# Pooling sums of q, k and v: one tensor_reduce each on VectorE in place of two additions each on GpSimd, in an attention and feed-forward kernel

## The chip, the cores and the metric

The kernel runs on one core of one Trainium2 chip. The metric is the device time of one execution in microseconds (us), lower is better. Times come from unprofiled runs, in rounds in which the kernels that are compared follow one another on the same chip; a profiled execution gives the trace from which all durations below are read. The core has a matrix engine (TensorE, PE in the rows; PEld is its weight load), VectorE (DVE), ScalarE (ACT), GpSimd (POOL), and SyncE (SP), whose queue here issues nearly all DMA transfers. Each engine works through its own queue in order and waits on semaphores for the others.

## The reference

The program is an attention followed by a token mix and a feed-forward layer, in fp32, for 8 batches, 8 heads, 576 positions and a head width of 64:

```python
# attention; factor = 4, Sd = 144
q_d = q.reshape(B, H, Sd, factor, D).mean(axis=3)      # the same for k_d and v_d
out_d = sm_attn(q_d, k_d, v_d)                         # softmax attention of the 144 pooled positions
out_up = np.repeat(out_d, factor, axis=2)
mask = np.abs(pos[:, None] - pos[None, :]) < factor    # local attention: 7 neighbours
out_local = softmax(where(mask, scale * q @ k.T, -1e9)) @ v
x = (out_up + out_local).transpose(0, 2, 1, 3).reshape(B, S, H * D)     # 8 x 576 x 512
# token mix of rank 32, then the feed-forward layer, 512 -> 2048 -> 512
u = x + (x.transpose(0, 2, 1) @ U @ V).transpose(0, 2, 1)
return u + np.maximum(u @ w_ch1, 0.0) @ w_ch2
```

The pooled means of q, k and v are where the change is: sums of four neighbouring positions (the factor 1/4 is folded in later).

## The kernel before, in words

**Products.** Every large product is done with operands split in a high and a low part (names ending in H and L), three matmuls for one: H by H, L by H, H by L. W1 and W2 are split on the chip: 32 chunks of 128x512 come in raw, and `convert` makes the two parts with seven instructions each (L341 and L351 on ACT, L342, L344, L347 and L349 on DVE, L354 on POOL); U goes the same way after the last chunk of W2.

**Work items.** A "pair" is two heads of one batch; there are 32, four for each batch. The first five ("early") use TensorE for most of their pooled and local attention, in buffers that later hold W2. The other 27 ("late") go through `late_global`: it loads q and k with the head width on the partitions (`gq`, `gT`, 128 x 576) and v in a grouped form (`vr`, 72 partitions x 2 x 4 x 64, one load for each head), sums fours into `smq`, `smk` (128x144) and `vs` (72x128), makes scores, softmax and the upsampled output, while `local_attn` does the seven-neighbour part on POOL (the product `Pt`, L799) and DVE (its sum over neighbours, L804). `mix_part` takes the output of a pair through U (`ps_hu`, L848) and V (`ps_u`, L863) into u, whose parts `uH` (ACT) and `uL` (POOL, L871) the feed-forward layer reads. Of the late pairs, pairs 5, 6 and 7 belong to batch 1, whose first pair is pair 4, an early one.

**Feed-forward.** For each batch, two tiles of 288 positions and 16 chunks of the hidden width: 12 matmuls into `ps_h` (L888), ACT makes `hH` (L895), DVE makes `hL` (L896), and three steps later 12 matmuls add into four accumulators (`acc`, L911). 256 such steps in all.

**What sets the order.** All instructions are first given to a planner, a list scheduler with a cost for each instruction, a priority for each (ten times the pair's number, with offsets) and the number of buffers of each tile. It fixes the order on every engine; the engines then run these fixed queues, and only semaphores decide when something starts. So a change of one instruction's engine or cost moves others on all engines. `hL` has the first place on DVE among what is ready. `gq`, `gT`, `vr` have one buffer each, `vs` two; so the load for a later pair waits until the sums of the pair before have read the buffer (and, for `gq` and `gT`, until its scores have).

**What the change touches.** For a late pair, `pool_halves` (L412 to L418) adds pairs of q, then pairs of these sums, in two POOL additions through a buffer `gh`; it does the same for k. For v, L510 adds in place (72x256), L512 adds the rest (72x128). That is eight POOL additions a pair:

Of the kernel before, what the change touches and what calls it, by code (L numbers as in the profile page):

```python
# [16 lines left out]
ALU = mybir.AluOpType  # L17
AX = mybir.AxisListType
# [35 lines left out]
class Plan:  # L54
# [6 lines left out]
    def buf(self, pool, shape, dt, name, tag=None, bufs=1):  # L61
        return Buf(self, pool, shape, dt, name, tag or name, bufs)

    def op(self, eng, dur, fn, r=(), w=(), prio=0.0, after=(), lat=None, move=0.0, at=0.0):
        o = Op()
        o.eng, o.dur, o.fn, o.prio, o.succ, o.ndep, o.ready = eng, dur, fn, prio, [], 0, at
        o.lat, o.move = LATENCY[eng] + SLACK * (SLACK_FROM <= prio < 1000) if lat is None else lat, move
        deps = set(after)
        bufs = []
        for k in r:  # L70
            b = k[0] if isinstance(k, tuple) else k
            bufs.append(b)
# [129 lines left out]
def attn_mix_ffn_kernel(ctx: ExitStack, tc, q, kp, vp, qT, kT, v, U, Ub, V, w1, w2, mask, band, eye, pat, pool, vw, vn, ident, outT):  # L202
    nc = tc.nc
    B, H, S, D = q.shape
    HP = H // 2
    NPOS = 9
    SPAD = kp.shape[2]
# [29 lines left out]
    op, buf = plan.op, plan.buf  # L237
# [30 lines left out]
    def pool_tt(n, fn, r, w, prio, ns=2.11, after=()):  # L268
        return op(POOL, 0.147 + n * ns / 1000.0, fn, r, w, prio, after)
# [29 lines left out]
    def ring(shape, name, n=2):  # L299
        if name not in kept:  # L300
            tiles = [early_pool.tile([128, *shape], F32, name=f"{name}{i}") for i in range(n)]
            for t in tiles:
                nc.vector.memset(t[:], 0.0)
            kept[name] = [0, [Kept(t) for t in tiles]]
        r = kept[name]
        r[0] += 1
        return r[1][(r[0] - 1) % n]
# [12 lines left out]
    for _ in range(2):  # L320
        m = kept_tile([NS, 2, KW], "ms_b")
        op(POOL, 0.4, lambda m=m: nc.gpsimd.tensor_copy(
            out=m()[:, :, :, KL:KW].rearrange("p r h k -> p (r h) k"),
            in_=pat_sb.unsqueeze(1).broadcast_to([128, 2 * NS, KW - KL])), ["pat"], [(m, "pat")], 0.1)
# [78 lines left out]
    def work(is_early, pool, shape, dt, name, tag=None, bufs=1):  # L403
        if is_early:
            return buf(early_pool, shape, dt, name, tag, 2)
        return buf(pool, shape, dt, name, tag, bufs)
# [5 lines left out]
    def pool_halves(raw, lo, out, e, prio):  # L412
        gh = work(e, glo, [128, SD, 2], F32, "gh")
        x4 = lambda: raw()[:, lo:lo + S].rearrange("p (j r) -> p j r", r=4)
        pool_tt(2 * SD, lambda: nc.gpsimd.tensor_tensor(
            out=gh(), in0=x4()[..., 0:2], in1=x4()[..., 2:4], op=ALU.add), [raw], [gh], prio, 1.65)
        pool_tt(SD, lambda: nc.gpsimd.tensor_tensor(
            out=out(), in0=gh()[..., 0], in1=gh()[..., 1], op=ALU.add), [gh], [out], prio, 1.75)  # L418

    def early_global(b, hp, up_s, prio, qt, kt, vn):  # L420
        sq = work(True, glo, [128, SD], F32, "smq")
        sk = work(True, glo, [128, SD], F32, "smk")
# [11 lines left out]
        vs = ring([4 * D], "vs_e")  # L434
# [13 lines left out]
        for hh in range(2):  # L448
            p = ps[hh]
            mx = work(True, glo, [QH, 2], F32, "mx")  # L450
            dve(288, lambda p=p, mx=mx: nc.vector.tensor_reduce(
                out=mx(), in_=view(p, SD), axis=AX.X, op=ALU.max), [p], [mx], prio)
# [14 lines left out]
        for hh in range(2):  # L467
# [13 lines left out]
            def a_mm(ET=ET, pa=pa, v=vsx[hh]):  # L481
# [6 lines left out]
                out=od()[:QH, 2 * hh:2 * hh + 2, :], in0=view(pa, D),  # L488
                in1=ri()[:, hh, :].unsqueeze(2).broadcast_to([QH, 2, D]), op=ALU.mult), [pa, ri], [(od, hh)], prio)
        for hh in range(2):  # L490
            dma(lambda hh=hh: nc.sync.dma_start(
                out=up_s()[hh].rearrange("(a p) d -> p a d", a=2), in_=od()[:, 2 * hh:2 * hh + 2, :]),
                [(od, hh)], [(up_s, hh)], prio, 40)

    def late_global(b, hp, up_s, prio):
        h0 = 2 * hp
        g = lambda shape, name, bufs=1: buf(glo, shape, F32, name, None, bufs)
        sq, sk = g([128, SD], "smq"), g([128, SD], "smk")
        qr, kr = g([128, S], "gq"), g([128, SPAD], "gT")
        load_t(qr, qT, b, h0, prio)  # L500
        load_t(kr, kT, b, h0, prio)
        pool_halves(qr, 0, sq, False, prio)
        pool_halves(kr, (SPAD - S) // 2, sk, False, prio)
        vss = []
        for hh in range(2):
            x, vs = g([QH, 2, 4, D], "vr"), g([QH, 2, D], "vs", 2)
            vss.append(vs)
            dma(lambda hh=hh, x=x: nc.sync.dma_start(
                out=x(), in_=v[b, h0 + hh].rearrange("(a p r) d -> p a r d", a=2, r=4)), [], [x], prio, 150)
            pool_tt(256, lambda x=x: nc.gpsimd.tensor_tensor(  # L510
                out=x()[:, :, 0:2, :], in0=x()[:, :, 0:2, :], in1=x()[:, :, 2:4, :], op=ALU.add), [x], [x], prio)
            pool_tt(128, lambda x=x, vs=vs: nc.gpsimd.tensor_tensor(  # L512
                out=vs(), in0=x()[:, :, 0, :], in1=x()[:, :, 1, :], op=ALU.add), [x], [vs], prio)
        s_s = buf(dram, [2, S, KL + 1], F32, "s_s", bufs=4)
        ps = late_scores(qr, kr, sq, sk, s_s, prio - 0.4)
        rs, rr, ri = (g([QH, 4], n) for n in ("rs", "rr", "ri"))
# [1 line left out]
        for hh in range(2):  # L518
            mx, nb = g([QH, 2], "mx", 2), g([QH, 2], "nb", 2)
            dve(288, lambda hh=hh, mx=mx: nc.vector.tensor_reduce(  # L520
                out=mx(), in_=pooled_view(ps[hh]), axis=AX.X, op=ALU.max), [ps[hh]], [mx], prio)
# [24 lines left out]
        out = lambda: pa()[:QH, :4 * D].rearrange("p (a d) -> p a d", a=4)  # L546

        def a_mm():
# [8 lines left out]
            out=od(), in0=out(), in1=ri().unsqueeze(2).broadcast_to([QH, 4, D]), op=ALU.mult), [pa, ri], [od], prio)  # L557
# [10 lines left out]
    def load_t(t, src, b, h0, prio):  # L568
        dma(lambda: nc.sync.dma_start(out=t(), in_=src[b, h0:h0 + 2].rearrange("h d s -> (h d) s")),
            [], [t], prio)  # L570
# [480 lines left out]
```

## Time and profile before

| | |
|---|---|
| median of the runs before | 1037.44 us (1034.21 to 1039.74, 3 runs) |
| profiled execution, its own time | 1038.36 us |
| its span | 1036.6 us |
| TensorE busy | 996.9 us (96%), mean granted clock 0.981 |
| VectorE busy | 529.8 us (51%), 1054 instructions |
| GpSimd busy | 557.2 us (54%), 567 instructions |
| ScalarE busy | 388.0 us (37%) |

How to read rows: a row of a group gives line, engine, operation, output<-input, shapes, count, then busy microseconds and the mean nanoseconds of one, then the idle time ahead of them and what ended it. A row of the windows view gives a stretch of the span, its length, then for each engine the busy microseconds (with the number of instructions), the granted TensorE clock (1.00 is full speed), the busy share of the DMA engines and GB/s. A row of a timeline gives start, duration, engine, line, operation, and in brackets the idle time before it with what it waited for. A row of the waits gives who waits, for what, total microseconds, how often, and the longest.

The span has three stages: the first 83 us (weights W1, the early pairs), the stretch from 83 to 168 us (W2 and U are loaded and converted, the feed-forward layer of batch 0 begins), and the long rest, in which the remaining batches follow one another.

### The profile page before, as it was taken

How to read it: one execution, taken by the hardware profiler on the slowest of the kernel's cores; microseconds unless marked ns; L12 is line 12 of the kernel's file. 1: busy time of each engine (PE TensorE's matmuls, PEld its weight loads, DVE VectorE, ACT ScalarE, POOL GpSimd, SP SyncE). 2: the span in 40 equal slices, each digit the busy share in tenths (PEclk: the TensorE clock that was granted, in tenths of full speed). 3: DMA queues.
4: the chain of work that ended last, by engine and by line, in shares of the span. 5: the costliest groups of instructions: out<-in, count | busy, mean ns of one | idle time of the engine just before them, and what ended most of it. 6: DMA issues, size and time to landing. Idle time of an engine off the chain costs nothing.

```text
span 1036.6 us, 26946 instructions
## 1 busy us (share of the span) xinstructions
PE 996.9 (96%) x10831; PEld 975.3 (94%) x10831; DVE 529.8 (51%) x1054; ACT 388.0 (37%) x1234; POOL 557.2 (54%) x567
## 2 busy tenths in 40 slices
PE   6778898999999999999999999999999999999998
PEld 5667888999999999999999999999999999999998
DVE  5997898655554545444475344534652544211111
ACT  3676554442443434443344244423443232111110
POOL 4854568788575656565585638762765625211010
PEclk9896999999999999999999999999999999999999
DMA  8866764753555545545555355624644242000000
GB/s 279 226 172 179 199 186 116 149 138 104 135 137 115 141 113 132 128 86 146 120 137 125 87 132 133 143 75 101 151 116 117 64 113 50 24 1 24 1 24 23
DMA packets 222612, 120.30 MB, mean 116 GB/s; under 512 B 175492, under 2 KB 198456, under 8 KB 222488
## 3 DMA queue, kind: packets, MB, share of 16 engines
q1 hardware_dynamic: 222488, 118.58, 45.5%
q8 instruction: 85, 1.39, 0.6%
q14 instruction: 39, 0.32, 0.1%
HBM read 87.78 MB, written 30.75 MB: 114 GB/s over the span
## 4 chain that ended last, share of the span: by engine, by line
PE 84%; DVE 7%; POOL 3%; issue 2%; DMA 2%; ACT 2%; SPq 0%; DVEq 0%; POOLq 0%; ACTq 0%
PE acc L911 36%; PE ps_h L888 35%; PE ps_a L552 2%; PE ps_b L719 2%; DVE c L347 2%; PE ps_hu L848 1%; DVE c L349 1%; PE ps_t L539 1%; DMA w2r<-in_W 1%; PE ps_b L726 1%; POOL Pt L799 1%; DVE c L342 1%; DVE c L344 1%; PE ps_a L484 1%; PE ps_v L431 1%
## 5 line engine op out<-in xcount | busy, mean ns | idle before, releaser
L911 PE MATMUL acc<-hH,W2H 128*128 128x288 f32 x1024 | 310.5, 303 | 0.0
L896 DVE SCALAR_TENSOR_TENSOR hL<-ps_h,hH 128x288 fp32r<-128x288 f32 x256 | 116.6, 455 | 378.6 <-ACT hH L895 378.0
L888 PE MATMUL ps_h<-uH,W1H 128*128 128x288 f32 x1024 | 304.3, 297 | 4.1 <-DVE hL L896 3.1
L911 PE MATMUL acc<-hH,W2L 128*128 128x288 f32 x1024 | 303.1, 296 | 2.6 <-POOL W2L L354 2.6
L888 PE MATMUL ps_h<-uL,W1H 128*128 128x288 f32 x1024 | 303.4, 296 | 1.2 <-POOL uL L871 1.2
L911 PE MATMUL acc<-hL,W2H 128*128 128x288 f32 x1024 | 302.6, 296 | 0.0
L888 PE MATMUL ps_h<-uH,W1L 128*128 128x288 f32 x1024 | 302.0, 295 | 0.0
L799 POOL TENSOR_TENSOR Pt<-vl,at 128x896 f32<-128x896 f32 (+1 forms) x135 | 233.4, 1809 | 115.1 <-DVE acc L804 61.1
L895 ACT ACTIVATE hH<-ps_h 128x288 fp32r<-128x288 f32 x256 | 105.1, 410 | 433.6 <-PE ps_h L888 433.5
L888 PEld LDWEIGHTS ps_h<-uH,W1H 128*128 128x128 f32 x1024 | 193.5, 189 | 5.4 <-DVE hL L896 3.8
L911 PEld LDWEIGHTS acc<-hH,W2L 128*128 128x128 f32 x1024 | 193.2, 189 | 3.5 <-POOL W2L L354 3.5
L888 PEld LDWEIGHTS ps_h<-uL,W1H 128*128 128x128 f32 x1024 | 193.4, 189 | 1.5 <-POOL uL L871 1.5
L911 PEld LDWEIGHTS acc<-hH,W2H 128*128 128x128 f32 x1024 | 193.3, 189 | 1.1
L888 PEld LDWEIGHTS ps_h<-uH,W1L 128*128 128x128 f32 x1024 | 193.7, 189 | 0.0
L911 PEld LDWEIGHTS acc<-hL,W2H 128*128 128x128 f32 x1024 | 193.7, 189 | 0.0
L804 DVE TENSOR_REDUCE acc<-Pt 128x128 f32<-128x1024 f32 (+1 forms) x135 | 144.7, 1103 | 4.7 <-POOL Pt L799 2.3
L871 POOL TENSOR_TENSOR uL<-xT,uH 128x288 fp32r<-128x288 f32 x56 | 44.1, 811 | 71.3 <-ACT uH L869 71.2
L921 POOL TENSOR_TENSOR o<-uH,uL 128x288 f32<-128x288 f32 x64 | 49.8, 816 | 54.2 <-DMA out_t<-o 54.2
L840 POOL TENSOR_TENSOR xL<-xL,xH 116x640 fp32r<-116x640 f32 x28 | 44.0, 1572 | 64.2 <-ACT xH L839 49.3
L510 POOL TENSOR_TENSOR vr<-vr 72x256 f32<-72x256 f32 x54 | 42.4, 785 | 46.9 <-DMA vr<-in_v 46.8
L793 ACT ACTIVATE Pt<-ul 128x128 f32<-128x128 f32 (+1 forms) x135 | 48.4, 441 | 21.3 <-DVE acc L804 20.0
L744 ACT ACTIVATE se<-ps_b 96x114 f32<-96x114 f32 x108 | 38.5, 357 | 47.1 <-PE ps_b L719 34.1
(129 smaller groups left out, 1106.9 us busy)
## 6 DMA issues: line engine op xcount, KB each, us to landing
vl<-in_vp SPq DMA_DIRECT2D x54, 240.0 KB
out_t<-o SPq DMA_DIRECT2D x64, 144.0 KB
w1r<-in_W SPq DMA_DIRECT2D x16, 512.0 KB
w2r<-in_W SPq DMA_DIRECT2D x16, 512.0 KB
Y<-x_s SPq DMA_DIRECT2D x112, 72.0 KB
gT<-in_kT SPq DMA_DIRECT2D x27, 291.0 KB
xL<-x_s SPq DMA_DIRECT2D x28, 280.0 KB
gq<-in_qT SPq DMA_DIRECT2D x27, 288.0 KB
```

The source lines that it names most:

```text
L510: pool_tt(256, lambda x=x: nc.gpsimd.tensor_tensor(out=x()[:, :, 0:2, :], in0=x()[:, :, 0:2, :], in1=x()[:, :, 2:4, :], op=ALU.add), [x], ...
L744: act(n * KL, lambda p=ps[hh], se=se, n=n, rows=rows: nc.scalar.activation(se()[rows, 0:n].rearrange("p r k -> p (r k)"), p()[rows, 0:n * ...
L793: act(n * D, lambda n=n, ps=ps, Pt=Pt: nc.scalar.activation(Pt()[:, :n, :, 7], ul()[:, ps, :], AF.Copy), [ul], [(Pt, 1)], prio, 0.16)
L799: nc.gpsimd.tensor_tensor(out=Pt()[:, :n, :, 0:7].rearrange("p s d o -> p o s d"), in0=win, in1=at()[:, ps, :].rearrange("p s o -> p o s") ...
L804: dve(8.5 * n * D, lambda n=n, ps=ps, Pt=Pt: nc.vector.tensor_reduce(out=acc()[:, ps, :], in_=Pt()[:, :n], axis=AX.X, op=ALU.add), [(Pt, 0 ...
L840: pool_tt(640, lambda: nc.gpsimd.tensor_tensor(out=xL(), in0=xL().bitcast(F32), in1=xH().bitcast(F32), op=ALU.subtract), [xL, xH], [xL], prio)
L871: pool_tt(TN, lambda uH=uH, uL=uL, uf=uf: nc.gpsimd.tensor_tensor(out=uL()[:, hp, :], in0=uf(), in1=uH()[:, hp, :].bitcast(F32), op=ALU.su ...
L888: nc.tensor.matmul(ps()[:, :TN], w[:, dc, fs], u()[:, dc, :], start=(n == 0), stop=(n == 3 * NDC - 1))
L895: last_h[i] = act(TN, lambda: nc.scalar.activation(hH(), ps()[:, :TN], AF.Relu), [ps], [hH], FIRST, 0.05)
L896: dve(TN, lambda: nc.vector.scalar_tensor_tensor(hL(), ps()[:, :TN], 0.0, hH().bitcast(F32), op0=ALU.max, op1=ALU.subtract), [ps, hH], [hL ...
L911: nc.tensor.matmul(ac[e]()[:, :TN], W2[w][:, fc, es], hx(), start=(fc == 0 and n == 0), stop=(fc == NFC - 1 and n == 2))
L921: pool_tt(TN, lambda e=e, o1=o1: nc.gpsimd.tensor_tensor(out=o1()[:, :TN], in0=uH()[:, e, :].bitcast(F32), in1=uL()[:, e, :].bitcast(F32), ...
```

## The change

For late pairs the two additions of q, of k and of each head's v become one VectorE instruction, a `tensor_reduce` that sums the innermost four elements: 128x144 from 128x576 for q and for k, 72x128 from 72x512 for each v (its view is permuted so that the four summed are innermost, 64 elements apart in the buffer). Early pairs keep `pool_halves`. The planner is told 576 and 512 elements as their cost on DVE.

```diff
+    def sum_fours(raw, lo, out, prio):
+        dve(S, lambda: nc.vector.tensor_reduce(
+            out=out(), in_=raw()[:, lo:lo + S].rearrange("p (j r) -> p j r", r=4), axis=AX.X, op=ALU.add),
+            [raw], [out], prio)
...
-        pool_halves(qr, 0, sq, False, prio)
-        pool_halves(kr, (SPAD - S) // 2, sk, False, prio)
+        sum_fours(qr, 0, sq, prio)
+        sum_fours(kr, (SPAD - S) // 2, sk, prio)
...
-            pool_tt(256, lambda x=x: nc.gpsimd.tensor_tensor(
-                out=x()[:, :, 0:2, :], in0=x()[:, :, 0:2, :], in1=x()[:, :, 2:4, :], op=ALU.add), [x], [x], prio)
-            pool_tt(128, lambda x=x, vs=vs: nc.gpsimd.tensor_tensor(
-                out=vs(), in0=x()[:, :, 0, :], in1=x()[:, :, 1, :], op=ALU.add), [x], [vs], prio)
+            dve(512, lambda x=x, vs=vs: nc.vector.tensor_reduce(
+                out=vs(), in_=x().rearrange("p a r d -> p a d r"), axis=AX.X, op=ALU.add), [x], [vs], prio)
```

Lines behind the new function are numbered five higher in the changed kernel, and three higher from the end of the v sums on: L804 becomes L807, L848 L851, L863 L866, L888 L891, L896 L899, L911 L914; the new reduces are L421 (q and k) and L515 (v).

Since the planner orders everything anew, the queues differ in more than the replaced rows. Three places follow.

VectorE, while W2 is converted (`c_...` is a chunk's working copy), the conversion of one chunk. Before:

```order
L342 TENSOR_SCALAR c_1867<-c_1867 128x512
L344 TENSOR_SCALAR c_1867<-c_1867 128x512
L347 SCALAR_TENSOR_TENSOR c_1867<-w2r,c_1867 128x512
L896 SCALAR_TENSOR_TENSOR hL<-ps_h,hH 128x288
L349 SCALAR_TENSOR_TENSOR c_1867<-w2r,c_1867 128x512
L342 TENSOR_SCALAR c_1942<-c_1942 128x512
```

Now:

```order
L342 TENSOR_SCALAR c_1869<-c_1869 128x512
L344 TENSOR_SCALAR c_1869<-c_1869 128x512
L515 TENSOR_REDUCE vs<-vr 72x128
L899 SCALAR_TENSOR_TENSOR hL<-ps_h,hH 128x288
L347 SCALAR_TENSOR_TENSOR c_1869<-w2r,c_1869 128x512
L421 TENSOR_REDUCE smq<-gq 128x144
L349 SCALAR_TENSOR_TENSOR c_1869<-w2r,c_1869 128x512
L421 TENSOR_REDUCE smk<-gT 128x144
L342 TENSOR_SCALAR c_1928<-c_1928 128x512
```

Three reduces of one pair now stand between the instructions of one chunk.

GpSimd, the last chunks of W2 and U (`Ust`). Before:

```order
L354 TENSOR_TENSOR W2L<-c_2252,W2H 128x512
L354 TENSOR_TENSOR W2L<-c_2298,W2H 128x512
L510 TENSOR_TENSOR vr<-vr 72x2x128
L799 TENSOR_TENSOR Pt<-vl,at 128x7x128
L354 TENSOR_TENSOR W2L<-c_2328,W2H 128x512
L512 TENSOR_TENSOR vs<-vr 72x128
L799 TENSOR_TENSOR Pt<-vl,at 128x7x128
L354 TENSOR_TENSOR W2L<-c_2420,W2H 128x512
L354 TENSOR_TENSOR Ust<-cu,Ust 116x5x32
```

Now:

```order
L354 TENSOR_TENSOR W2L<-c_2249,W2H 128x512
L354 TENSOR_TENSOR W2L<-c_2272,W2H 128x512
L802 TENSOR_TENSOR Pt<-vl,at 128x7x128
L354 TENSOR_TENSOR W2L<-c_2342,W2H 128x512
L802 TENSOR_TENSOR Pt<-vl,at 128x7x128
L354 TENSOR_TENSOR W2L<-c_2373,W2H 128x512
L354 TENSOR_TENSOR Ust<-cu,Ust 116x5x32
```

The additions of v are gone from between them; the rest keeps its order. On TensorE, the first `ps_hu` (of pair 4), which reads `Ust`, had 216 matmuls of L888 and 180 of L911 ahead of it, and now has 228 and 195.

TensorE, from the end of batch 0 to batch 1 (`ps_hu` and `ps_u` here are those of pair 7, the last of batch 1). Before, the end of that stretch; `ps_hu` stands further up, with twelve L911 between it and `ps_u`:

```order
L911 MATMUL acc_2685<-hH,W2L 128x288
L863 MATMUL ps_u<-Vst,stk 128x288 x2
L911 MATMUL acc_2693<-hH,W2H 128x288
L911 MATMUL acc_2693<-hL,W2H 128x288
L911 MATMUL acc_2693<-hH,W2L 128x288
L911 MATMUL acc_2699<-hH,W2H 128x288
L911 MATMUL acc_2699<-hL,W2H 128x288
L911 MATMUL acc_2699<-hH,W2L 128x288
L888 MATMUL ps_h<-uH,W1H 128x288
```

Now:

```order
L914 MATMUL acc_2675<-hH,W2H 128x288
L914 MATMUL acc_2675<-hL,W2H 128x288
L914 MATMUL acc_2675<-hH,W2L 128x288
L851 MATMUL ps_hu<-xH,Ust 64x128 x5
L851 MATMUL ps_hu<-xL,Ust 64x128 x5
L866 MATMUL ps_u<-Vst,stk 128x288 x2
L542 MATMUL ps_t<-ident_sb,E 72x72 x8
L891 MATMUL ps_h<-uH,W1H 128x288
```

The eighteen matmuls of batch 0 that stood between these steps now all come before `ps_hu`; a transpose of the next pair (`ps_t`) stands ahead of the first `ps_h` of batch 1. On GpSimd at that place the two last `uL` still stand behind two `Pt` of 128x896, and now behind a third of 128x448 too.

## The prediction

> **What bounds the kernel now.** I read the windows first, by the stages at which TensorE's busy time changes.
>
> ```profile
> core 0: us, PE busy (x) PEld busy (x) DVE busy (x) ACT busy (x) POOL busy (x), PEclk, DMA share, GB/s
> 25.00:50.00 25.00, 19.97 (x414) 16.80 (x413) 23.51 (x48) 14.68 (x49) 20.65 (x23) 0.80 0.83 228
> 50.00:75.00 25.00, 17.52 (x338) 14.07 (x343) 23.30 (x46) 18.84 (x59) 13.53 (x13) 0.96 0.60 169
> 82.60:168.00 85.40, 73.77 (x935) 69.35 (x933) 76.37 (x130) 47.36 (x132) 51.80 (x46) 0.90 0.67 179
> 168.00:171.90 3.90, 3.88 (x23) 3.88 (x24) 3.22 (x11) 1.88 (x10) 3.90 (x5) 0.57 0.34 98
> 171.90:229.30 57.40, 57.40 (x647) 56.88 (x646) 34.90 (x67) 25.77 (x84) 45.86 (x43) 1.00 0.60 143
> 229.30:236.00 6.70, 4.70 (x34) 4.23 (x33) 5.28 (x12) 2.71 (x7) 6.62 (x10) 1.00 0.52 140
> 236.00:900.00 664.00, 663.54 (x7168) 658.04 (x7167) 321.97 (x651) 244.18 (x810) 393.66 (x399) 1.00 0.47 114
> ```
>
> From 236 to 900 us TensorE is idle for 0.46 us, from 171.9 to 229.3 not at all, at full clock. There only TensorE's instructions set the pace, and the change leaves these alone. GpSimd's 393.66 and VectorE's 321.97 of 664 us are not limits. What can move the end are the idle times and lowered clocks before 236: 12.5 us idle in 25 to 75, 11.6 in 82.6 to 168, 2.0 at 229.3 to 236. VectorE is nearly full in the first two (46.8 of 50, 76.4 of 85.4). The whole run's averages (VectorE 51%, GpSimd 54%) hide this.
>
> The waits of TensorE in the first 250 us (total, times, longest) name who is late there; three of them bear on the change:
>
> ```profile
> PE ps_h L888 <- DVE hL L896: 3.1, 3, 1.4
> PE ps_hu L848 <- POOL Ust L354: 2.5, 1, 2.5
> PE ps_h L888 <- POOL uL L871: 1.2, 1, 1.2
> ```
>
> The chain of waits, cut to 82 to 168, gives the engine behind them:
>
> ```profile
> by line: DVE c L347 13.5%; DMA w2r<-in_W 11.6%; issue 10.9%; DVE c L342 8.1%; DVE c L344 8.0%; DVE c L349 7.6%; DMA Y<-x_s 6.7%; POOL W2L L354 4.8%; PE acc L911 4.4%; DVE hL L896 3.3%; ACT c L341 2.4%; PE ps_h L888 2.2%; DVE cu L347 2.0%; S
> ```
>
> VectorE's conversion lines (L347, L342, L344, L349) are 37% of it and with hL and U about 43%; GpSimd's W2L is 5%, the loads 12%.
>
> **The change part by part.** *Removed:* 8 GpSimd additions for each of 27 pairs, 216. In the saturated stages they cost nothing now. In the stage of W2 they are, as groups of that window,
>
> ```profile
> L510 POOL TENSOR_TENSOR vr<-vr 72x256 f32<-72x256 f32 x4 | 4.7, 1184 | 0.0
> L415 POOL TENSOR_TENSOR gh<-gq 128x288 f32<-128x288 f32 x3 | 3.3, 1116 | 0.0
> L512 POOL TENSOR_TENSOR vs<-vr 72x128 f32<-72x128 f32 x5 | 2.7, 547 | 0.9 <-PE ps_a L552 0.8
> L415 POOL TENSOR_TENSOR gh<-gT 128x288 f32<-128x288 f32 x3 | 2.4, 812 | 0.1
> L417 POOL TENSOR_TENSOR smq<-gh 128x144 f32<-128x144 f32 x3 | 1.8, 610 | 0.2
> L417 POOL TENSOR_TENSOR smk<-gh 128x144 f32<-128x144 f32 x3 | 1.8, 589 | 0.1
> ```
>
> 16.7 us, 32% of GpSimd's 51.80 there.
>
> *Added:* 108 reduces on VectorE, none of which the trace has. The nearest rows are the reduce of the local attention and, for strided words, a conversion that reads every second word:
>
> ```profile
> L804 DVE TENSOR_REDUCE acc<-Pt 128x64 f32<-128x512 f32 x27 | 18.2, 675 | 1.1 <-POOL Pt L799 1.1
> L804 DVE TENSOR_REDUCE acc<-Pt x135: 643/1209/1222, 165.2 to 872.5; 128x128 f32<-128x1024 f32 x108, 128x64 f32<-128x512 f32 x27
> L347 DVE SCALAR_TENSOR_TENSOR c<-w2r,c x16: 672/808/1748, 97.2 to 161.8; 128x512 int32<-128x512 int32 x16
> L342 DVE TENSOR_SCALAR c<-c x32: 407/420/4018, 15.0 to 156.9; 128x512 f32<-128x512 f32 x32
> ```
>
> The median of the source row, 1209 ns, is that of the 1024 elements (108 of its 135), the group row gives 675 for 512. So 512 more cost 534 ns, 1.043 each: 576 elements take 0.742 us, 512 take 0.675. For v the four lie 64 words apart; L347 with strided words still goes through 512 in 672 ns, so I take no surcharge. Each next start comes about 0.08 us before the end (in the timeline below one lasts from 156.90 to 160.92, and the next starts at 160.84), so a reduce holds VectorE for 0.66 or 0.60 us. Two of each make 2.83 us per pair, 76.5 for 27 pairs, and VectorE goes from 530 to about 606 us.
>
> In the *saturated stages* (94 of the 108 reduces, the other 14 are in A and B; 67 us onto VectorE's 357 of 721) the cost is 0: the reduces hide behind TensorE's work as long as hL, which stands behind them on VectorE, keeps its slack. Nine matmuls take 1.19 us (229.35 to 230.54 below), so a step's twelve take 1.59. `ps_h` has two buffers, so one is needed again after three such groups, 4.8 us; hH and hL take 0.41 and 0.46 of it:
>
> ```profile
> L896 DVE SCALAR_TENSOR_TENSOR hL<-ps_h,hH 128x288 fp32r<-128x288 f32 x256 | 116.6, 455 | 378.6 <-ACT hH L895 378.0
> L895 ACT ACTIVATE hH<-ps_h 128x288 fp32r<-128x288 f32 x256 | 105.1, 410 | 433.6 <-PE ps_h L888 433.5
> ```
>
> 3.9 us remain, and one reduce ahead costs 0.7. Without that cover it would be up to the 67 us.
>
> *Term A, 25 to 75 us:* pair 5's four reduces, 2.5 us on a VectorE with 3.2 us left. Bounds 0 and +2.5; TensorE has 12.5 us of idle here that other waits cause, so nearer nothing: **+0.5**.
>
> *Term B, W2 stage:* ten reduces (three of q, three of k and four of v stand in the new order between pair 5's and U's end), 6 x 0.66 + 4 x 0.60 = 6.4 us onto VectorE. Against it, the same stage shows VectorE held up while GpSimd works:
>
> ```profile
> 156.90 4.02 DVE L342 TENSOR_SCALAR c<-c 128x512 f32<-128x512 f32 x1
> 160.84 0.21 DVE L772 TENSOR_REDUCE lmx<-ms 128x9 f32<-128x63 f32 x1
> ...
> 156.39 1.19 POOL L510 TENSOR_TENSOR vr<-vr 72x256 f32<-72x256 f32 x1
> ...
> 160.60 0.64 POOL L512 TENSOR_TENSOR vs<-vr 72x128 f32<-72x128 f32 x1
> ...
> L347 DVE SCALAR_TENSOR_TENSOR c<-w2r,c 128x512 int32<-128x512 int32 x16 | 17.5, 1094 | 0.2
> L349 DVE SCALAR_TENSOR_TENSOR c<-w2r,c 128x512 int32<-128x512 int32 x16 | 14.2, 886 | 0.1
> L342 DVE TENSOR_SCALAR c<-c 128x512 f32<-128x512 f32 x18 | 13.0, 723 | 4.8 <-ACT c L341 4.7
> ```
>
> An instruction that takes 0.41 at its median took 4.02 while GpSimd ran four instructions in a row (the first and the last are shown; the product Pt and a W2L stand between). These two, the first and the last, are the ones removed. Over their least (672 ns, 672 taken for L349 too, 407) the three groups are stretched by 6.8, 3.4 and 5.7 us, 15.9; a third of GpSimd's work goes, so 32% of it, 5.1 us, comes back. Bounds +6.4 (nothing returned, all on the path) and -5.1 (all returned, reduces in VectorE's 9.0 idle us). VectorE is 43% of the chain: 0.43 x (6.4 - 5.1) = **+0.6**.
>
> [...]
>
> *Term C, U:* the wait for Ust (2.5 us) is followed by 3.9 us at clock 0.57, which lose 0.43 x 3.9 = 1.7. Now 12 + 15 = 27 more feed-forward matmuls stand ahead of ps_hu in TensorE's queue, at 0.132 each 3.6 us of cover; the price falls to nothing only if U's chain does not end later itself, and the ten reduces stand ahead of it on VectorE. Bounds -4.2 and 0 (if W2's chain ends as much later); between, nearer the cover: **-2.0**.
>
> *Term D, batch 0 to 1:* now
>
> ```profile
> 226.01 0.47 PE L848 MATMUL ps_hu<-xH,Ust 116*64 116x128 f32 x5
> 228.26 0.43 PE L863 MATMUL ps_u<-Vst,stk 128*128 128x288 f32 x2
> 229.35 0.29 PE L888 MATMUL ps_h<-uH,W1H 128*128 128x288 f32 x1
> 230.54 0.29 PE L888 MATMUL ps_h<-uH,W1H 128*128 128x288 f32 x1
> 232.06 0.40 PE L888 MATMUL ps_h<-uL,W1H 128*128 128x288 f32 x1 [1.23 <-POOL uL L871]
> ...
> 227.40 0.28 DVE L853 TENSOR_TENSOR stk<-ps_hu,stk 32x128 fp32r<-32x128 f32 x1 [2.13 <-ACT stk L856]
> 228.90 0.45 DVE L866 TENSOR_TENSOR xT<-ps_u,xT 128x288 f32<-128x288 f32 x1
> 230.36 2.34 DVE L804 TENSOR_REDUCE acc<-Pt 128x128 f32<-128x1024 f32 x2
> ```
>
> Twelve and six matmuls of batch 0 stand in the two steps hu to ps_u to ps_h; afterwards none, so both are bare. The ten hu matmuls are through about 0.7 after the first row's start, at 226.73; stk ends at 227.68: 0.95 idle. Behind ps_u the next is ps_t, which needs the two PSUM buffers that xT gives back, and VectorE has one L804 reduce (2.34 for two, so 1.2) ahead of xT (0.45): with a quarter for the hand-overs 1.9. Together 2.85 against 2.0 now, +0.85, the least; with the removed uL wait gone but a low clock after it (1.7, as behind Ust) and a late xL, up to +5. I take **+1.5**, nearer the least, because the two idles are parted by ps_u.
>
> [...]
>
> Sum: 0.5 + 0.6 - 2.0 + 1.5 = +0.6. On the profiled execution's 1038.36 that is 1039.0; the median of the runs is 0.9 lower, so 1038.0. The rivals below are counted from the median, 1037.4.
>
> **The rivals.** *VectorE bounds the W2 stage (slower).* All 6.4 us enter the path, nothing returns since the remaining GpSimd work meets the same VectorE instructions, Ust stays late: 0.5 + 6.4 + 0 + 1.5 = +8.4, 1045.8. For it: 76.37 of 85.40; against: 9.0 us idle, 57% of the chain elsewhere. It decides once VectorE in this stage is busy for more than 85.4 less its waits for loads. *The reduces are held up as L347 is (slower):* 1094 - 672 = 0.42 each, 10 x 0.42 = 4.2 more, 1050.0. Against: L804's 1222. [...] *VectorE freed (faster):* -5.1 comes back, the reduces fit the idle 9.0, Ust is covered with its low clock (-4.2), A and D as forecast: -7.3, 1030.1. For it: the row of 4.02, and 27 matmuls of cover. *Loads (slower):* GpSimd waited for v,
>
> ```profile
> POOL vr L510 <- DMA vr<-in_v: 46.8, 9, 8.6
> ```
>
> which costs nothing there; on VectorE, hL would stand behind it. Nine waits beyond a slack of 3.9 leave at least 46.8 - 35.1 = 11.7, 1049. Against: 45 of the 54 sums of v found their data there. The SP queue issues the same loads after the same releases, so I add nothing for them. *No effect but another order* is inside the forecast, since TensorE sets 57.4 and 664 us of the span by itself.
>
> **How the numbers follow.** Forecast 0.53, own range 1032.5 to 1042.5, which is what a measurement of this kernel calls the same (0.5% is 5.2 us); freed 0.22; VectorE-bound 0.17; held up 0.04; loads 0.04. So faster 0.22, same 0.53, slower 0.25. To leave no more than 2 in 10 out, the range takes in the centres of the first two rivals and stops before the last two: 1029.5 to 1046.5.
>
> **What would show it.** [...] L347 and L342 nearer their least in 82 to 168; the wait of ps_hu for Ust gone and the clock at 1.00 behind it; at the batch boundary two bare waits (ps_u for stk, ps_t for xT) of 2 to 4 us; after that TensorE still full to 900 us. I am wrong if TensorE waits for hL again and again after 236 us, if the W2 stage ends more than 5 us earlier or later, or if a reduce waits for a load with hL behind it.

## The result, and the profile after

The changed kernel takes 1044.44 us (median of 17 runs, 1040.26 to 1050.55) against 1038.31 us before (17 runs beside it, 1034.21 to 1042.17). The ratio is 1.0063, with a 95% interval of 1.0048 to 1.0079: slower by 6 us. The profiled execution took 1047.78 us (span 1046.0), 3.3 above its median, so its trace holds somewhat more than the typical loss.

The same stages in the windows view of the changed kernel, with the batch boundary cut where its idle time begins and ends:

```profile
core 0: us, PE busy (x) PEld busy (x) DVE busy (x) ACT busy (x) POOL busy (x), PEclk, DMA share, GB/s
82.60:168.00 85.40, 73.52 (x949) 69.89 (x948) 78.88 (x142) 47.31 (x127) 37.37 (x25) 0.90 0.66 178
168.00:171.90 3.90, 3.31 (x30) 3.07 (x29) 3.87 (x12) 3.27 (x15) 3.90 (x5) 1.00 0.76 190
171.90:228.20 56.30, 56.30 (x725) 55.31 (x723) 40.01 (x74) 24.99 (x81) 35.33 (x28) 1.00 0.68 146
228.20:244.00 15.80, 9.72 (x56) 9.23 (x56) 11.55 (x25) 7.49 (x28) 8.86 (x8) 0.68 0.67 177
244.00:900.00 656.00, 653.19 (x6979) 647.38 (x6979) 375.97 (x719) 237.97 (x788) 301.33 (x230) 1.00 0.47 112
```

The low clock behind Ust (0.57 before) is gone, TensorE is saturated from 171.9 as before, and then comes a row that the kernel before does not have: from 228.2 to 244 us TensorE is idle for 6.1 us, at a mean clock of 0.68. Before, the idle time at this place was 2.0 us at clock 1.00.

What was late there, by the timeline of TensorE:

```profile
231.33 0.53 PE L851 MATMUL ps_hu<-xH,Ust 116*64 116x128 f32 x5 [3.10 <-ACT E L528]
231.69 0.46 PE L851 MATMUL ps_hu<-xL,Ust 116*64 116x128 f32 x5
234.30 0.82 PE L866 MATMUL ps_u<-Vst,stk 128*128 128x288 f32 x2 [2.15 <-DVE stk L856]
235.96 1.17 PE L542 MATMUL ps_t<-ident_sb,E 72*72 72x72 f32 x8 [0.84 <-DVE xT L869]
```

The bare steps that the prediction named are there, each with its wait. The first is new: ps_hu, a matmul of the token mix, waits for an exponential (L528) of pair 11, because the scores of pair 11 (ps_b) came shortly before it on TensorE and hold the two PSUM buffers that ps_hu shares with them.

The chain of waits, cut to 222 to 237 us, shows whose work the path consists of (start, duration, what):

```profile
221.20 5.05 DMA Y<-x_s
226.28 0.78 DVE xT L841
227.06 1.10 DVE acc L807
228.16 0.72 DVE mx L523 x2
...
229.45 0.73 DVE o L927 x2
230.18 0.69 DVE ms L776
230.86 0.73 DVE o L927 x2
231.60 0.99 DVE vs L515
...
232.72 1.12 DVE acc L807
...
233.87 0.28 DVE stk L856
...
234.43 1.11 DVE acc L807
235.54 0.37 DVE xT L869
...
235.96 1.05 PE ps_t L542 x7
```

VectorE waits at the head of its queue for a load (Y), and then works without a pause until 235.9. The maxima that pair 11's buffers wait for (mx), the part of pair 7's mix (stk) and its sum (xT) stand between other pairs' sums. Only 0.99 us of these 9.6 is one of the new reduces.

The prices of the new instructions, as groups of the whole run:

```profile
L515 DVE TENSOR_REDUCE vs<-vr 72x128 f32<-72x512 f32 x54 | 58.1, 1076 | 2.9 <-DMA vr<-in_v 2.8
L421 DVE TENSOR_REDUCE smk<-gT 128x144 f32<-128x576 f32 x27 | 20.0, 741 | 0.6 <-DMA gT<-in_kT 0.6
L421 DVE TENSOR_REDUCE smq<-gq 128x144 f32<-128x576 f32 x27 | 19.9, 736 | 0.1
```

The v reduces by their source line (least, median and largest ns):

```profile
L515 DVE TENSOR_REDUCE vs<-vr x54: 1008/1075/1110, 51.5 to 811.2; 72x128 f32<-72x512 f32 x54
```

And the groups of the stage of W2 for the conversions that GpSimd held up before (in the kernel before, of the 32 of these two lines, the 17 that began while GpSimd worked took up to 1.75 us, the other 15 took 0.67 to 0.69):

```profile
L347 DVE SCALAR_TENSOR_TENSOR c<-w2r,c 128x512 int32<-128x512 int32 x16 | 15.2, 948 | 0.1
L349 DVE SCALAR_TENSOR_TENSOR c<-w2r,c 128x512 int32<-128x512 int32 x16 | 12.7, 792 | 0.0
```

q and k cost what the local sums let one expect (0.74 us), v costs 1.08 us instead of 0.675. None is held up by GpSimd: the longest v reduce is 35 ns over the median, and the 26 that began while GpSimd worked took 1.06 to 1.11 us, the other 28 took 1.01 to 1.09. These two conversion lines take 15.2 and 12.7 us where they took 17.5 and 14.2. Of the other two, L342 fell from 13.0 to 10.0 us and L344 rose from 10.6 to 12.7, so the four together take 50.6 us instead of 55.3.

How far the change is ahead or behind can be followed by when the first matmul of a feed-forward step starts (us; step 32 is the first of batch 1):

| step | before | changed | difference |
|---|---|---|---|
| 18 | 172.1 | 165.6 | -6.5 |
| 26 | 202.0 | 199.2 | -2.8 |
| 30 | 218.2 | 215.5 | -2.7 |
| 36 | 241.4 | 251.6 | +10.2 |
| 72 | 375.8 | 383.5 | +7.7 |
| 136 | 613.6 | 624.7 | +11.1 |
| 255 | 1026.5 | 1035.9 | +9.4 |

So in this pair of executions step 30 comes 2.7 us earlier. One execution of each kernel doesn't put that beyond chance: in numbers 1, 3, 6, 7 and 12 below, which keep the order of before up to there, step 30 starts 0.7 to 5.9 us later than in the kernel before. Between steps 30 and 36 the changed kernel takes 36.1 us instead of 23.2 and loses it all and more. Of these 12.9 us, 4.1 are idle time (6.1 against 2.0). In one part of the stretch the clock was low:

```profile
232.18:242.42 10.24, 7.28 (x33) 6.97 (x34) 6.87 (x14) 3.61 (x12) 3.29 (x5) 0.50 0.75 196
```

TensorE works for 7.28 us there at half clock, by an estimate a loss of 3.6 us (half of 7.28; for the idle time in between a low clock is not counted). Measured, the matmuls of ps_h start 0.24 us apart there (237.50 to 242.06 us) and 0.13 at full clock right behind it (242.62 to 243.82), a loss of 45%, so 3.6 is rather high. The last 5.2 us fit the matmuls of pairs that stand earlier in the new order: between these two steps the changed kernel has 252 matmuls outside the feed-forward layer, the kernel before 20. They are not lost: by step 72 2.5 us of them have come back. The sum to the end: -2.7 + 4.1 + 3.6 + 2.4 (idle time in the long rest, 2.81 against 0.46) = 7.4 of the 9.4 us between the two profiled executions; the other 2.0 are not accounted for.

### The profile page after: what moved, and what is told of

It is laid out like the page before. It is cut to its first block, busy times and chain, and to the rows that moved or that the text cites. A ratio compares the mean times of both kernels' runs of the same rounds, so it can differ in the third digit from the quotient of the medians.

```text
span 1046.0 us, 26766 instructions
## 1 busy us (share of the span) xinstructions
PE 997.0 (95%) x10831; PEld 975.7 (93%) x10831; DVE 599.0 (57%) x1162; ACT 387.7 (37%) x1234; POOL 437.9 (42%) x351
## 4 chain that ended last, share of the span: by engine, by line
PE 79%; DVE 11%; DMA 4%; ACT 2%; issue 2%; POOL 1%; SPq 1%; DVEq 0%; ACTq 0%; POOLq 0%
PE ps_h L891 34%; PE acc L914 34%; PE ps_a L555 2%; PE ps_b L722 2%; PE ps_hu L851 1%; DVE c L347 1%; DVE c L349 1%; DMA w2r<-in_W 1%; DVE acc L807 1%; PE ps_t L542 1%; POOL Pt L802 1%; DVE hL L899 1%; PE ps_b L729 1%; DVE vs L515 1%; DVE c L344 1%
## 5 line engine op out<-in xcount | busy, mean ns | idle before, releaser
L914 PE MATMUL acc<-hH,W2H 128*128 128x288 f32 x1024 | 309.7, 302 | 1.6 <-ACT W2H L351 1.0
L891 PE MATMUL ps_h<-uH,W1H 128*128 128x288 f32 x1024 | 306.6, 299 | 1.9 <-DVE hL L899 1.8
L899 DVE SCALAR_TENSOR_TENSOR hL<-ps_h,hH 128x288 fp32r<-128x288 f32 x256 | 116.2, 454 | 332.1 <-ACT hH L898 331.2
L891 PE MATMUL ps_h<-uL,W1H 128*128 128x288 f32 x1024 | 304.9, 298 | 0.0
L914 PE MATMUL acc<-hH,W2L 128*128 128x288 f32 x1024 | 303.0, 296 | 0.9 <-POOL W2L L354 0.8
L891 PE MATMUL ps_h<-uH,W1L 128*128 128x288 f32 x1024 | 303.5, 296 | 0.0
L914 PE MATMUL acc<-hL,W2H 128*128 128x288 f32 x1024 | 303.0, 296 | 0.0
L891 PEld LDWEIGHTS ps_h<-uH,W1H 128*128 128x128 f32 x1024 | 194.6, 190 | 3.0 <-DVE hL L899 2.7
L914 PEld LDWEIGHTS acc<-hH,W2H 128*128 128x128 f32 x1024 | 192.8, 188 | 3.2 <-ACT W2H L351 1.2
L891 PEld LDWEIGHTS ps_h<-uH,W1L 128*128 128x128 f32 x1024 | 195.2, 191 | 0.0
L891 PEld LDWEIGHTS ps_h<-uL,W1H 128*128 128x128 f32 x1024 | 194.9, 190 | 0.0
L914 PEld LDWEIGHTS acc<-hH,W2L 128*128 128x128 f32 x1024 | 192.7, 188 | 1.4 <-POOL W2L L354 1.3
L914 PEld LDWEIGHTS acc<-hL,W2H 128*128 128x128 f32 x1024 | 193.1, 189 | 0.0
L807 DVE TENSOR_REDUCE acc<-Pt 128x128 f32<-128x1024 f32 (+1 forms) x135 | 145.4, 1100 | 11.6 <-POOL Pt L802 6.5
L515 DVE TENSOR_REDUCE vs<-vr 72x128 f32<-72x512 f32 x54 | 58.1, 1076 | 2.9 <-DMA vr<-in_v 2.8
```

What stands on the lines that cost most here:

```text
L515: dve(512, lambda x=x, vs=vs: nc.vector.tensor_reduce(out=vs(), in_=x().rearrange("p a r d -> p a d r"), axis=AX.X, op=ALU.add), [x], [vs] ...
L807: dve(8.5 * n * D, lambda n=n, ps=ps, Pt=Pt: nc.vector.tensor_reduce(out=acc()[:, ps, :], in_=Pt()[:, :n], axis=AX.X, op=ALU.add), [(Pt, 0 ...
L891: nc.tensor.matmul(ps()[:, :TN], w[:, dc, fs], u()[:, dc, :], start=(n == 0), stop=(n == 3 * NDC - 1))
L899: dve(TN, lambda: nc.vector.scalar_tensor_tensor(hL(), ps()[:, :TN], 0.0, hH().bitcast(F32), op0=ALU.max, op1=ALU.subtract), [ps, hH], [hL ...
L914: nc.tensor.matmul(ac[e]()[:, :TN], W2[w][:, fc, es], hx(), start=(fc == 0 and n == 0), stop=(fc == NFC - 1 and n == 2))
```

## The experiments

Two theories stood at first. "Order": the loss is the new order of the queues, above all at the end of batch 0. "Load": VectorE's added work delays others wherever it stands. In every run all sums are computed. Since the order follows from what the planner is told, and the engine from what is issued, the two can be parted: the planner can be shown one kernel while the other's instructions are issued.

**1. The order of before, all reduces on VectorE.** TensorE's queue is that of before, row for row.

```diff
+        pool_tt(2 * SD, lambda: None, [raw], [gh], prio, 1.65)
+        pool_tt(SD, lambda: nc.vector.tensor_reduce(...), [gh, raw], [out], prio, 1.75)
...
+            pool_tt(256, lambda: None, [x], [x], prio)
+            pool_tt(128, lambda x=x, vs=vs: nc.vector.tensor_reduce(...), [x], [vs], prio)
```

> The planner sees the kernel before, so every queue keeps the order of before; only the 108 sums of late q, k and v run as one reduce each on VectorE, at the place in the program where the second addition stood (the first addition is left out). Theory 'order': the loss of the changed kernel (+6.1 us in the runs) is the new order at the end of batch 0, and the additions' move itself saves some 3 us before it; expects 1034 to 1039 beside 1038 before, with no wait of ps_hu over 1 us at the batch boundary. Rival 'load': VectorE's added work (599 against 530 us, v reduces of 1.08 us) delays hL and the rest wherever it stands; expects 1042 or more.

Measured: 1044.17 us, ratio 1.0051 (1.0035 to 1.0068). By the time, the rival "load" is right; by the trace, "order" is right on its place: steps 30 to 36 take 23.2 us as before, although VectorE carries all 108 reduces. The profiled execution (1040.94 us) was the fastest of its runs, so most of the loss isn't in its trace; the run was repeated as number 12.

**2. The order of the changed kernel, the additions on GpSimd.**

```diff
+        def adds():
+            nc.gpsimd.tensor_tensor(out=gh(), in0=x4()[..., 0:2], in1=x4()[..., 2:4], op=ALU.add)
+            nc.gpsimd.tensor_tensor(out=out(), in0=gh()[..., 0], in1=gh()[..., 1], op=ALU.add)
+        dve(S, adds, [raw], [gh, out], prio)
...
+            dve(512, adds, [x], [x, vs], prio)
```

> The planner sees the changed kernel, so every queue keeps the order of the changed one; the sums themselves run as the two additions on GpSimd as before. Theory 'order': the wait of ps_hu and the low clock behind it stay without a single new reduce; expects 1043 to 1050. Rival 'load': without VectorE's added work the loss is gone; expects 1036 to 1040.

Measured: 1062.54 us, ratio 1.0231 (1.0213 to 1.025). The loss stays without a single new reduce (steps 30 to 36: 35.9 us, 6.4 of them idle, and 10.2 us at half clock as in the changed kernel), so "load" falls for this place. That it is worse by 18 us than the changed kernel was expected by neither. The rest of it lies in long stalls later, of which this is the longest (VectorE, GpSimd, then TensorE, by the timelines of this run):

```profile
703.96 7.63 DVE L786 SCALAR_TENSOR_TENSOR ms<-sc,mask_sb 128x63 f32<-128x63 f32 x1
711.51 1.21 DVE L820 TENSOR_REDUCE acc<-Pt 128x128 f32<-128x1024 f32 x1
...
702.27 3.86 POOL L815 TENSOR_TENSOR Pt<-vl,at 128x896 f32<-128x896 f32 x2
705.92 1.60 POOL L856 TENSOR_TENSOR xL<-xL,xH 116x640 fp32r<-116x640 f32 x1
707.44 1.14 POOL L815 TENSOR_TENSOR Pt<-vl,at 128x448 f32<-128x448 f32 x1
708.37 3.14 POOL L937 TENSOR_TENSOR o<-uH,uL 128x288 f32<-128x288 f32 x4
...
714.65 0.61 PE L904 MATMUL ps_h<-uH,W1H 128*128 128x288 f32 x1 [4.09 <-DVE hL L912]
```

An instruction on 63 elements takes 7.63 us, until GpSimd's row of instructions without a gap (eight are shown) ends at 711.5; hL stands behind it, and TensorE waits 4.09 us.

**3. The change from pair 12 on** (80 reduces; the order of before up to batch 1).

```diff
-        sum_fours(qr, 0, sq, prio)
...
+        if prio >= 120:
+            sum_fours(qr, 0, sq, prio)
...
+        else:
+            pool_halves(qr, 0, sq, False, prio)
```

> The change for pairs 12 to 31 only, 80 of the 108 reduces; pairs 5 to 11 keep the additions on GpSimd, and TensorE's order at the end of batch 0 is that of before. Theory 'order': expects 1036 to 1040, no difference. Rival 'load': three quarters of the loss stay, 1042 to 1043.

Measured: 1040.18 us, ratio 1.0020 (1.0004 to 1.0036), between the two, nearer "order". Three quarters of the reduces cost 2 us when the early part keeps its order; so about 4 of the 6 us go with the pairs 5 to 11, as far as the two parts simply add. The order behind the early part is new here too, so the 2 us are not those of the reduces alone.

**4. The change for pairs 5 to 7 only** (`prio < 80`; 12 reduces).

> The change for pairs 5, 6 and 7 only, 12 of the 108 reduces. TensorE's order at the end of batch 0 has ps_hu, ps_u and the first ps_h of batch 1 next to each other as in the changed kernel, without the ps_t between. Theory 'order': a part of the loss, bare waits at this place of 3 to 6 us, against 3 us saved in the stage of W2; expects 1038 to 1046. Rival 'load': a ninth of the loss, 1038 to 1039, and no new wait at this place.

Measured: 1039.06 us, ratio 1.0013 (0.9997 to 1.0028): no difference clear of noise, and by the time alone at the edge of "load" too. The trace speaks for "order", since new waits are there: it is 2.6 us ahead at step 30, then takes 27.1 us for steps 30 to 36, with ps_u waiting 1.05 us and ps_h 1.28, and is 1.3 us behind at step 36.

**5. The scores of pair 11 held back until ps_hu of pair 7.**

```diff
-        op(PE, 1.1, mm, [qr, kr, sq, sk], ps, prio)
+        op(PE, 1.1, mm, [qr, kr, sq, sk], ps, prio, [last_mix[(1, 3)]] if 109 < prio < 110 else ())
```

> The changed kernel with one more dependency: the score matmuls (ps_b) of pair 11 wait for ps_hu of pair 7. TensorE's queue is that of the changed kernel up to the end of batch 0, where ps_hu now comes before these scores and finds its PSUM buffer free. Theory 'boundary' (the changed kernel loses its time where ps_hu waits for the two PSUM buffers that the scores of pair 11 hold until ACT's and VectorE's work on them is done): the wait of 3.1 us and part of the low clock behind it go; expects 1036 to 1041, and under 3 us of idle at this place. Rival 'load' (VectorE's longer queue costs everywhere): 1043 to 1046.

Measured: 1044.36 us, ratio 1.0063 (1.0045 to 1.0082): no gain. TensorE, and VectorE in the same stretch:

```profile
224.69 0.51 PE L852 MATMUL ps_hu<-xL,Ust 116*64 116x128 f32 x5 [1.00 <-POOL xL L844]
228.48 0.82 PE L867 MATMUL ps_u<-Vst,stk 128*128 128x288 f32 x2 [3.28 <-DVE stk L857]
...
226.85 1.04 DVE L515 TENSOR_REDUCE vs<-vr 72x128 f32<-72x512 f32 x1
227.81 0.20 DVE L783 RECIPROCAL lrl<-lse 128x9 f32<-128x9 f32 x1
228.05 0.28 DVE L857 TENSOR_TENSOR stk<-ps_hu,stk 32x128 fp32r<-32x128 f32 x1
```

The wait for the PSUM buffers is gone, as meant, and turned into a wait of 3.28 us one step later: ps_u waits for stk, which stands behind a softmax of another pair and a new v reduce. So the PSUM buffers as the only cause fall; the place is right (32.5 us for steps 30 to 36, 5.0 of them idle against 6.1 in the changed kernel), but what limits it is the whole chain of pair 7's mix through VectorE's and ACT's queues. The profiled execution (1042.15 us) was the fastest of its runs.

**6 and 7. The order of before, with only q and k, or only v, as reduces.** The edits are the halves of number 1.

> Every queue in the order of before; late q and k as reduces on VectorE (54 of 0.74 us), v as before on GpSimd. In the run with all reduces in this order 6.4 us were lost. If the loss goes with VectorE's time: 40 of 98 us are added here, expects +2.6 us, 1040 to 1041. If it is the long reduce of v (1.08 us): no loss, 1036 to 1039.

> Every queue in the order of before; v as reduces on VectorE (54 of 1.08 us), q and k as before on GpSimd. By VectorE's time: 58 of 98 us, +3.8 us, 1041 to 1042. If the long reduce of v is the cause: the whole loss, 1043 to 1045.

Measured: q and k 1038.33 us, ratio 1.0000 (0.9988 to 1.0012); v 1037.99 us, ratio 0.9995 (0.9979 to 1.0010). Neither rule of the expectations holds: each half is free, both together cost 5 to 6 us (numbers 1 and 12). VectorE has room for 40 or for 58 us more of reduces in this order, not for 98.

**8. The change for q and k alone, planned anew** (v stays on GpSimd).

> The change for q and k alone, planned anew; v stays on GpSimd. At the end of batch 0 ps_hu, ps_u and ps_h stand next to each other, but the scores of pair 11 come after them. Theory 'boundary': no wait of 3 us for ps_hu, expects 1035 to 1040. Rival 'load': 40 of the 98 us on VectorE, 1040 to 1041.

Measured: 1047.87 us, ratio 1.0096 (1.0077 to 1.0114), beyond both. The same 54 reduces that cost nothing in the order of before cost 10 us in an order of their own. Steps 30 to 36 take 27.1 us, 2.7 of them idle, and later GpSimd holds up VectorE as in number 2 (5.67 us beside 5.61 of GpSimd's work):

```profile
770.64 5.67 DVE L775 SCALAR_TENSOR_TENSOR ms<-sc,mask_sb 128x63 f32<-128x63 f32 x1
...
770.75 5.61 POOL L804 TENSOR_TENSOR Pt<-vl,at 128x896 f32<-128x896 f32 x3
...
779.43 0.37 PE L916 MATMUL acc<-hH,W2H 128*128 128x288 f32 x1 [3.25 <-ACT hH L900]
```

Here hH stands on ACT behind work that waits for ms, and TensorE waits for hH.

**9 and 10. The kernel before with another order.** No instruction is changed; the planner is told another price for the additions of v.

```diff
-                out=x()[:, :, 0:2, :], in0=x()[:, :, 0:2, :], in1=x()[:, :, 2:4, :], op=ALU.add), [x], [x], prio)
+                out=x()[:, :, 0:2, :], in0=x()[:, :, 0:2, :], in1=x()[:, :, 2:4, :], op=ALU.add), [x], [x], prio, 1.75)
```

(the second addition likewise; 2.5 in number 10).

> The kernel before, with not one instruction changed; only the planner is told a lower price for the additions of v on GpSimd (1.75 instead of 2.11 ns an element), so that it makes another order. Theory 'new order' (a good part of the 6 us is the price of leaving the order of before, whatever the instructions): expects 1041 to 1046. Theory 'work' (VectorE's added work): 1036 to 1039.

> As the run above, with a higher price (2.5 ns an element); at the end of batch 0 TensorE's ps_hu, ps_u and ps_h stand next to each other as in the changed kernel. Theory 'new order': 1041 to 1048, with bare waits of 3 us or more there. Theory 'work': 1036 to 1039.

Measured: 1042.98 us, ratio 1.0038 (1.0019 to 1.0058), and 1043.68 us, ratio 1.0044 (1.0022 to 1.0066). Both lie within "new order": these two orders cost about 4 us although not one instruction differs. Steps 30 to 36 take 26.3 and 28.2 us. The waits there stay under the 3 us that was expected of number 10: 1.64, 1.41 and 0.76. In the trace of number 9 a good part of the loss stands elsewhere: it is 5.5 us late at step 0, 2.6 at step 30 and 6.4 at the end.

**11. The changed kernel, with the planner told the measured price of a v reduce.**

```diff
-            dve(512, lambda x=x, vs=vs: nc.vector.tensor_reduce(
+            dve(900, lambda x=x, vs=vs: nc.vector.tensor_reduce(
```

> The changed kernel, with the planner told what a v reduce takes (900 elements, 1.0 us, instead of 512 elements, 0.60 us). Theory 'price' (the planner's order is bad because it holds the v reduce for 0.4 us too cheap): 1036 to 1040. Theory 'boundary' (ps_hu, ps_u, ps_t and ps_h stand bare next to each other here too): 1042 to 1047.

Measured: 1042.96 us, ratio 1.0033 (1.0014 to 1.0052), at the lower end of "boundary" and not "price". The middle is 0.3% better than the changed kernel's; their intervals meet, so a gain from the right price is possible and not shown. Steps 30 to 36 take 30.7 us, in a profiled execution (1039.40 us) that was the fastest of its runs.

**12. Number 1 once more.**

> All reduces on VectorE in the order of before, once more: the first profile of it was of its fastest execution. Expects 1042 to 1046 again, with a profile in which od, mx or xT come late behind reduces after 236 us and TensorE waits for them with ps_b, or in which the first 170 us are longer by 3 us or more; if it is 1036 to 1039 this time, the first measurement was the exception and the reduces cost nothing in this order.

Measured: 1045.70 us, ratio 1.0059 (1.0039 to 1.0080): the loss is real. This profile (1045.90 us) is a typical one. It is 3.2 us behind before by step 18 (2.8 of these at step 0, which in other runs with this order lies 0.9 to 5.1 us later than before), takes 2.7 us more between steps 28 and 30, where ps_hu waits 1.48 us for xL, and 1.4 between steps 56 and 72. This last one is the same, within 0.1 us, in both profiles of this kernel and nearly absent in numbers 6 and 7 (0.4 and 0.1). Here, VectorE's rows and TensorE's:

```profile
359.59 0.81 DVE L930 TENSOR_TENSOR o<-acc,o 128x288 f32<-128x288 f32 x2
360.32 0.45 DVE L872 TENSOR_TENSOR xT<-ps_u,xT 128x288 f32<-128x288 f32 x1
360.68 0.74 DVE L423 TENSOR_REDUCE smq<-gq 128x144 f32<-128x576 f32 x1
361.34 0.45 DVE L872 TENSOR_TENSOR xT<-ps_u,xT 128x288 f32<-128x288 f32 x1
361.71 1.06 DVE L518 TENSOR_REDUCE vs<-vr 72x128 f32<-72x512 f32 x1
362.69 1.21 DVE L810 TENSOR_REDUCE acc<-Pt 128x128 f32<-128x1024 f32 x1
363.81 0.74 DVE L423 TENSOR_REDUCE smk<-gT 128x144 f32<-128x576 f32 x1
364.47 0.44 DVE L902 SCALAR_TENSOR_TENSOR hL<-ps_h,hH 128x288 fp32r<-128x288 f32 x1
364.84 1.80 DVE L810 TENSOR_REDUCE acc<-Pt 128x128 f32<-128x1024 f32 x2
366.56 0.41 DVE L562 TENSOR_TENSOR od<-ps_a,ri 72x256 f32<-72x256 f32 x1
...
367.03 0.43 PE L732 MATMUL ps_b<-smk,smq 64*32 64x144 f32 x7 [0.96 <-DVE od L562]
```

VectorE works 7.3 us without a gap; od, at its end, gives a PSUM buffer back, and TensorE, whose next instruction needs it, waits 0.96 us. Without the v reduce (1.06) or without the two of q and k (1.48) the row is shorter by more than this wait, and in the traces of numbers 6 and 7 the wait is gone. That shows for 1.4 of the 5 to 6 us why each half is free and the whole is not; for the rest it is not shown.

All steps 30 to 36 together (us, from the profiled executions; in brackets TensorE's idle time in them):

| order of before there | | a new order there | |
|---|---|---|---|
| before | 23.2 (2.0) | changed | 36.1 (6.1) |
| 1 and 12, all reduces | 23.3, 23.2 (2.1, 2.0) | 2, additions on GpSimd | 35.9 (6.4) |
| 6, q and k | 23.1 (1.9) | 5, scores held | 32.5 (5.0) |
| 7, v | 23.2 (2.0) | 11, true price | 30.7 (3.2) |
| 3, from pair 12 on | 23.2 (2.0) | 10 and 9, no instruction changed | 28.2, 26.3 (4.1, 3.4) |
| | | 4 and 8 | 27.1, 27.1 (2.6, 2.7) |

Every order other than the first takes 3 to 13 us longer over these steps, with reduces or without, and the first takes no longer with all of them. Not all of that is loss: 0.6 to 4.4 us are idle time beyond the 2.0 of before, a low clock adds up to 3.6 by the estimate above (nothing in numbers 9 and 10), and the rest are matmuls that the new orders place there.

## Why the prediction was right and wrong, step by step

The measured 1044.4 us lies in the range, but the likeliest case, "the same", is missed: the middle is 0.63% slower, 6.1 us where the sum gave +0.6. That the range holds it is luck: its upper end comes from the rival in which VectorE bounds the stage of W2, and that is not what happened.

- *TensorE's saturated stages bound the kernel; what moves the end lies before 236 us.* Mostly right: from 244 to 900 us 2.81 us of 656 are idle (0.46 before). The cover for the reduces was looked for in hL alone. hL did keep its slack; the waits that came instead are od's (1.9 us once), a reader of the two shared PSUM buffers, as in number 12, and two for a v sum itself (0.8). The list of what stands behind a reduce on VectorE was incomplete: mx, xT and od free buffers for TensorE too.
- *Price of a reduce.* Right for q and k (0.742 against 0.739 to 0.742 measured), wrong for v (0.675 against 1.076). L347 as the row for strided words misled: its words are two apart (512 elements in 672 ns at its least), the reduce's four are 64 apart (512 in 1008 ns at its least). 54 x 0.4 = 22 us more of reduces, though number 7 shows that v alone in the order of before costs nothing. VectorE's busy time came to 599.0 us all the same, under the 606 forecast: neighbouring instructions overlap (by 0.07 to 0.09 us in the rows of number 12), and the durations of its other instructions sum to 13 us less than before.
- *Term A, +0.5.* Not to be told from chance: step 0 starts 0.4 us earlier here, and between 4.5 earlier and 5.5 later in the experiments, the 5.5 in a run without any reduce (number 9).
- *Terms B and C, +0.6 and -2.0.* The direction was right in this trace: the four conversion lines fell by 4.7 us in the stage of W2, where 5.1 was forecast for three of them, the wait for Ust and the low clock behind it are gone, and A to C make -2.8 us at step 26 where -0.9 was forecast. Part of it is chance: in numbers 3 and 7 the same wait for Ust (2.52 and 2.57 us) left the clock at 1.00, so the 1.7 us that term C estimated for the low clock aren't lost in every execution.
- *Term D, +1.5, at most +5.* This is the step that failed. The two waits that it named came, ps_u for stk (2.15 us) and ps_t for xT (0.84). Their sum, 2.99, is near the 2.85 forecast, but by luck: the forecast had 0.95 and 1.9. What the term left out is the wait ahead of them, 3.10 us of ps_hu for the PSUM buffers of pair 11's scores; and the low clock, taken as 1.7 us at most, cost an estimated 3.6. Together 4.1 us more idle and 3.6 of clock, 7.7 us. That the term lies nearer its least because ps_u parts the two idle times was not shown: here the clock stayed at 0.50 over the parted 2.15 and 0.84, while in number 10 it stayed at 1.00 over 1.64, 1.41 and 0.76. It was built from the durations of stk and xT with one reduce ahead, from the kernel before, in which VectorE had 2.1 us free at that place. The new order fills VectorE there for 9.6 us, after a wait at the head of its queue for Y, and puts pair 11's scores ahead of ps_hu. Both stand in the new order, which was read for TensorE and GpSimd here but not far enough for VectorE.
- *The rivals.* None of them is what happened. "VectorE bounds the W2 stage" gave the nearest time (1045.8) for a wrong reason: that stage did not become slower. "Held up as L347" falls: the longest reduces took 1110 ns (v) and 754 ns (q and k). "Loads" has its mechanism in the wait for Y (2.3 us once), not in v (2.8 us in three).
- *"No effect but another order is inside the forecast."* This is the sentence that was wrong in kind: another order alone costs 4 us in both cases that were tried (numbers 9 and 10).

Where the 6 us of the runs go is settled in part. Shown: a new order by itself costs some 4 us in two cases; at the end of batch 0 the changed kernel loses by its order and not by its reduces, since number 2 loses as much there without any of them, and numbers 1 and 12 nothing with all of them; all reduces in the old order cost 5 to 6 us, of which 1.4 are seen as a full VectorE queue ahead of od. Open: the two do not add up (4 and 5 to 6 against 6), so how much of the changed kernel's loss belongs to its order and how much to VectorE's load can't be said; in numbers 1 and 12 the rest of the loss isn't at a fixed place; and whether the order of before is an unusually good one, from which almost any other would lose, was not tested. No version tried was faster than the kernel before; numbers 6 and 7 equal it, and number 4 can't be told from it.

## What to carry to other kernels

In a kernel whose queues are ordered by a planner, a changed instruction is two changes: its own price and a new order of everything. Measure them apart, by issuing the new instructions in the old order, and the old ones in a newly made order; here the second alone was worth 0.4%. When work moves to an engine at half load, list every instruction behind it that frees a buffer for the bounding engine, not only the one on the main path, and read the moved order of that engine at each place where the bounding engine has no other work to fill in.

## What the runs showed of the hardware

- In the changed kernel a `tensor_reduce` of four elements to one costs 739 to 742 ns (medians of q and k, 691 to 754 in all) for 576 elements that lie next to each other and 1075 ns (1008 to 1110) for 512 that lie 64 words apart: 1.29 against 2.1 ns an element, not the same as had been taken.
- Some of VectorE's instructions took longer where they began while GpSimd worked. In the kernel before, the 128 that convert the chunks of W1 and W2 (L342, L344, L347, L349) took up to 4.02 us where they began so (57 of them) and 0.36 to 0.69 where GpSimd stood (71); `ms` from `sc` (L770) up to 2.92 (15) and 0.20 to 0.22 (12). In the changed kernel the same are up to 2.13 (49) and at most 0.69 (79), up to 1.69 (14) and at most 0.22 (13). One such instruction was held over several of GpSimd's in a row, in the long rest too: `ms` took 7.63 us in number 2 and 5.67 in number 8, and ended within 0.1 us of GpSimd's row of instructions both times. The reduces were not held: those of v took 1.06 to 1.11 us where they began while GpSimd worked (26) and 1.01 to 1.09 elsewhere (28), those of q and k at most 0.75 in both cases.
- The length of a gap alone doesn't say whether the clock falls. In the changed kernel it fell to 0.50 behind a gap of 3.10 us and stayed there over two more (2.15 and 0.84) for 10.24 us in all. In number 10 gaps of 1.64, 1.41 and 0.76 at the same place left it at 1.00 (first row), while in number 4 gaps of 1.05, 0.31 and 1.28 were followed by 3.41 us at half clock (second row). Behind one wait of 2.50 for Ust the kernel before ran at 0.57 for 3.9 us, and behind the same wait of 2.52 number 3 ran at 1.00 (third row):

```profile
226.00:236.00 10.00, 5.93 (x39) 5.28 (x40) 7.12 (x10) 2.46 (x7) 9.84 (x12) 1.00 0.28 83
233.02:236.43 3.41, 3.41 (x15) 3.41 (x16) 1.63 (x4) 0.41 (x1) 3.41 (x6) 0.50 0.37 117
168.80:176.00 7.20, 6.78 (x58) 6.55 (x59) 5.74 (x15) 3.66 (x15) 7.20 (x8) 1.00 0.40 125
```
